# Mixing the keys of batches 2 and 3 with a stationary block matrix and relaying them through a scratch in HBM

## The chip, the cores and the metric

The kernel runs on one core of a Trainium2 chip. The metric is the device time of one execution in microseconds (us). A single execution also gives the span of its profile, which is the time from the first to the last instruction and about 2 us shorter. A run counts as slow when it lies over 1.5% above the fastest run of the same kernel; "same" means within 2%.

## The reference, cut to what matters

```python
# q, k, v: (4 batches, 8 heads, 768 positions, 64); 8 blocks of 96 positions
P = sort_net                      # 5 Sinkhorn rounds make it (nearly) doubly stochastic
k_sorted = einsum('bhij,bhjcd->bhicd', P, k_b)      # mix the 8 blocks of keys, per head
v_sorted = einsum('bhij,bhjcd->bhicd', P, v_b)
attn = softmax(scale * q_b @ k_sorted_b^T)          # attention inside each block
x    = (attn @ v_sorted_b)  ->  (3072 tokens, 512)
out  = (silu(x @ w_gate) * (x @ w_val)) @ w_out     # w_gate, w_val: 512 x 1536
```

The kernel cuts the 3072 tokens into eight stages of 384. Stage n is one pass of gate, value and output projection over the tokens of half a batch, and while it runs, the attention of a later half batch is computed in between. "Stage 2" below runs from the first gate matmul of its tokens to the first of stage 3. Changed is how the keys of batches 2 and 3 are mixed, which falls into stage 2. Their first use is in stage 4.

## The kernel before: the parts that matter here

The matmuls here sum over the partitions. The natural layout of the keys of a pair of batches is (batch, head, block) on the 128 partitions and (position, 64 dims) along the row. For the scores, the 64 dims must lie on the partitions. The kernel before mixes and turns in one step: each matmul takes 128 x 64 keys as the stationary operand and the mixing matrix as the moving one, so the dims come out on the partitions.

```python
def kq_chunk(b, at, n, eng, tag):           # n positions; two output halves of 64 dims
    ...
    for lc in range(n):
        for two in range(2):
            nc.tensor.matmul(tp[two * D:(two + 1) * D, lc, :],
                             lhsT=kq_tiles[b][:, at + lc, :], rhs=rm[:, two], start=True, stop=True)
    drain(eng, dst[:, :, at:at + n], tp.transpose([0, 2, 1]))
```

Pairs of such chunks, 64 matmuls, stand together three times in stage 2. The queries of batches 2 and 3 need no mixing. They already go through HBM and a transposing DMA:

```python
def q_cast(b):      # HBM to HBM, float32 to bfloat16, positions outermost
    nc.gpsimd.dma_start(out=q_scr[b - 2].rearrange("s (h d) -> s h d", d=D),
                        in_=q[b].rearrange("h s d -> s h d"))
def q_dma(b):
    dst = kqt_tile("q")[:, (b - 2) * GI * C:(b - 1) * GI * C]
    nc.sync.dma_start_transpose(out=dst.rearrange("p (g s) -> p g s", g=H2), in_=q_scr[b - 2])
```

The attention outputs of each unit (tile st) reach the feed-forward through another transposing DMA on the same queue, SyncE's:

```python
def x_dma(b, u):
    ...
    nc.sync.dma_start_transpose(out=xts[(b, half)][:, g, :].rearrange("p (i c) -> p i c", c=C),
                                in_=sts.pop((b, u)).rearrange("p i two d -> p (i two d)"))
...
merge(ffn(2), units(1, range(4, 8), (0.0, 5.5)) + kqs("p", (13.0, 16.2, 19.4))
      + [(13.0, lambda: q_dma(2)), (16.4, lambda: q_dma(3))])
```

The softmax here doesn't subtract the row's maximum and nothing guards it: scores larger than these inputs give would overflow.

Of the kernel before, what the change touches and what calls it, by code (L numbers as in the profile page):

```python
# [10 lines left out]
BF16 = mybir.dt.bfloat16  # L11
# [6 lines left out]
def kernel(  # L18
# [11 lines left out]
    nc = tc.nc  # L30

    B, H, S, D = q.shape
    NB = sort_net.shape[-1]
    C = S // NB
    BH = B * H
    H2 = H // 2
# [7 lines left out]
    R = H * NB  # L44
# [10 lines left out]
    natp = ctx.enter_context(tc.tile_pool(name="natp", bufs=2))  # L55
# [13 lines left out]
    warm_sb = const.tile([128, 512], BF16)  # L69
# [9 lines left out]
    nc.vector.memset(e_all[:, :, 4 * C:], 0.0)  # L79

    dram = ctx.enter_context(tc.tile_pool(name="dram", bufs=1, space=bass.MemoryType.DRAM))
    q_scr = [dram.tile([S, H * D], BF16, name=f"q_scr{b}") for b in range(2, B)]
    kq_tiles = {}
    v_tiles = {}
# [32 lines left out]
    def copy_v(eng, pair, rows, s, n=4, d0=0, d1=D):  # L117
        cs = slice(s * (C // n), (s + 1) * (C // n))
        dst = vch3[rows, d0:d1, cs]
        src = v_tiles[pair][rows, cs, d0:d1]  # L120
        if eng is nc.scalar:
            eng.copy(dst, src.transpose([0, 2, 1]))
        else:
            eng.tensor_copy(dst, src.transpose([0, 2, 1]))  # L124
# [4 lines left out]
    ET = mybir.EngineType  # L129
    man = tc.manual_schedule(engines={ET.PE, ET.Pool, ET.DVE, ET.Activation})  # L130
# [23 lines left out]
    rmix = {b: const.tile([128, 2, H, NB], BF16, name=f"rmix{b}") for b in (0, 1, "p")}  # L154
# [21 lines left out]
    def pair_tile(name, tag):  # L176
        return psum.tile([128, 1024], FP32, name=name, tag=tag)

    def bank_tile(name, tag="gen"):
        return psum.tile([128, 512], FP32, name=name, tag=tag, bufs=3 if tag == "gen" else 1)  # L180
# [28 lines left out]
    def drain(eng, dst, src):  # L209
        if eng == "v":  # L210
            nc.vector.tensor_copy(dst, src)  # L211
        else:
            nc.scalar.copy(dst, src)  # L213
# [3 lines left out]
    def kqt_tile(b):  # L217
        if b not in kqts:
            kqts[b] = kqp.tile([128, 2 * H2 * NB * C + 32], BF16, name=f"kqt{b}", tag="kqt")
        return kqts[b]  # L220

    GI = H2 * NB
# [26 lines left out]
    def v_pair_chunk(pair, at, n, eng, tag):  # L249
# [6 lines left out]
                             start=True, stop=True)  # L256
        drain(eng, dst[:, :, at:at + n], tp[0:C].transpose([0, 2, 1]))

    es, sts, xts = {}, {}, {}
    ecount = [0]  # L260

# [30 lines left out]
    def qk(b, u, tag="b"):  # L292
        exps(b, u, *scores(b, u, tag))
# [48 lines left out]
# [3 lines that stand above are left out]
# [66 lines left out]
    idle_ps = bank_tile("idle_ps", "x")  # L411

    def fill(tile, n):
        for _ in range(n):
            nc.tensor.matmul(tile, lhsT=warm_sb[:, 0:128], rhs=warm_sb, start=True, stop=True)

    for _ in range(109):
        nc.tensor.matmul(idle_ps[0:32, 0:32], lhsT=warm_sb[:, 0:32], rhs=warm_sb[:, 0:32],
                         start=True, stop=True)
    for it, n in ((1, 3), (2, 4), (3, 4), (4, 4)):  # L420
        nc.tensor.matmul(idle_ps[0:NB, 0:NB], lhsT=rowreds[it][:, :, 0], rhs=rowreds[it][:, :, 0],
                         start=True, stop=True)
# [10 lines left out]
    def mix_of(dst, b, w):  # L433
        lo = (b % 2) * R
        nc.vector.tensor_tensor(dst, mask[lo:lo + R].unsqueeze(2).to_broadcast([R, H, NB]),
                                w[lo:lo + R].transpose([0, 2, 1]), op=ALU.mult)
# [21 lines left out]
    for b in range(1, B):  # L458
        rows = highr if b % 2 else lowr
        mix_of(rmix["p"][rows, b % 2] if b > 1 else rmix[1][rows, 0], b, w_sb[:, :, b // 2])  # L460
    fill(idle_ps, 3)
    qk(0, 0, "a")
    qk(0, 1, "b")
    qk(0, 2, "gen")
    idle_ps = bank_tile("idle_ps")
# [40 lines left out]
    gate_out(0, 1, first[2])  # L506
    nc.vector.tensor_copy(rmix[1][lowr, 1].rearrange("p h i -> p (h i)"), ident[lowr, lowr])
    man.__exit__(None, None, None)
    man = tc.manual_schedule(engines={ET.PE, ET.Pool})
    man.__enter__()  # L510

    def units(b, us, ats):
        us = list(us)
        todo = []
        for n, at in enumerate(ats):
            u, u2 = us[2 * n:2 * n + 2]
            held = []
            todo.append((at, lambda u=u, u2=u2, held=held: (qk(b, u, "b"), held.append(scores(b, u2, "a")))))
            todo.append((at + 1.3, lambda u2=u2, held=held: exps(b, u2, *held[0])))
            for w, tag, t in ((u, "b", 1.9), (u2, "a", 3.6)):  # L520
                if b == 0 or b == 1 and u < H2:
                    todo.append((at + t, lambda w=w, tag=tag: av(b, w, tag)))
                    todo.append((at + t + 3.1, lambda w=w: drain("v", *xtr(b, w))))
                else:
                    todo.append((at + t, lambda w=w, tag=tag: (av(b, w, tag), x_dma(b, w))))
        return todo

    def kqs(b, ats):
        return [(at, lambda n=n: (kq_chunk(b, n * 32, 16, "v", "b"), kq_chunk(b, n * 32 + 16, 16, "s", "a")))
                for n, at in enumerate(ats)]  # L530

    def vs(f, size, ats):
        return [(at, lambda m=m: f(1, m * size, size, "sv"[m % 2], "ba"[m % 2])) for m, at in enumerate(ats)]

    def merge(main, side):
        done, k = 0.0, 0
        side = sorted(side, key=lambda t: t[0])
        for c, f in main:
            f()
            done += c  # L540
            while k < len(side) and side[k][0] <= done:
                side[k][1]()
                k += 1
        while k < len(side):
            side[k][1]()
            k += 1

    def ffn(n):
        todo = []
        for m in range(NFC):  # L550
            if n > 0 or m > 1:
                todo.append((0.65, lambda m=m: gate(n, m)))
            if n > 0 or m > 0:
                todo.append((0.65, lambda m=m: value(n, m)))
            ends = (5, 8, 11) if n == 1 else (3, 7, 11)
            if n > 0 and m in ends:
                for part in range(3):
                    todo.append((0.87, lambda t3=ends.index(m), part=part: outp(n - 1, t3, part)))
        return todo
# [8 lines left out]
    both = slice(0, 128)  # L568
    merge(ffn(0), units(0, range(4, 8), (0.0, 5.6)))
    merge(ffn(1), vs(v_chunk, 16, (2.2, 3.1, 4.0, 4.9)) + kqs(1, (5.8, 8.0, 10.2)) + units(1, range(4), (11.3, 15.8)))  # L570
    for s in range(4):
        copy_v(nc.gpsimd, 1, both, s)
    nc.vector.memset(kqt_tile("p")[:, 2 * GI * C:], 0.0)
    merge(ffn(2), units(1, range(4, 8), (0.0, 5.5)) + kqs("p", (13.0, 16.2, 19.4))
          + [(13.0, lambda: q_dma(2)), (16.4, lambda: q_dma(3))])
    merge(ffn(3), vs(v_pair_chunk, 8, [1.15 * n for n in range(8)]) + units(2, range(4), (9.8, 14.0)))
    merge(ffn(4), units(2, range(4, 8), (0.0, 8.0)))
    merge(ffn(5), units(3, range(4), (0.0, 8.0)))
    merge(ffn(6), units(3, range(4, 8), (0.0, 8.0)))
# [36 lines left out]
```

## Time and profile before

| | before |
|---|---|
| time, median of 4 runs in the rounds with the change | 250.97 us (250.1 to 253.65) |
| span of the profiled run | 248.4 us |
| TensorE (PE) busy | 237.0 us, 95% |
| stage 2, stage 3 | 29.38 us, 29.69 us |

The prediction below shows the busy shares, the chain and the costs of the pieces. Two more rows of the page matter for what follows. In both, each digit is a fortieth of the span: the clock that TensorE was granted, and the mean busy share of the 16 DMA engines, in tenths.

```profile
PEclk9999999999999999999999999999999999999999
DMA  5949999999999399110112121112111111100122
```

### The profile page before, as it was taken

How to read it: one execution, taken by the hardware profiler on the slowest of the kernel's cores; microseconds unless marked ns; L12 is line 12 of the kernel's file. 1: busy time of each engine (PE TensorE's matmuls, PEld its weight loads, DVE VectorE, ACT ScalarE, POOL GpSimd, SP SyncE). 2: the span in 40 equal slices, each digit the busy share in tenths (PEclk: the TensorE clock that was granted, in tenths of full speed). 3: DMA queues.
4: the chain of work that ended last, by engine and by line, in shares of the span. 5: the costliest groups of instructions: out<-in, count | busy, mean ns of one | idle time of the engine just before them, and what ended most of it. 6: DMA issues, size and time to landing. Idle time of an engine off the chain costs nothing.

```text
span 248.4 us, 5998 instructions
## 1 busy us (share of the span) xinstructions
PE 237.0 (95%) x2528; PEld 141.9 (57%) x2552; DVE 157.6 (63%) x332; ACT 110.4 (44%) x187; POOL 52.7 (21%) x47
## 2 busy tenths in 40 slices
PE   6698999999999999999999999999999999999995
PEld 5285565665555556666655655565555565555543
DVE  6787689785665775857558647755764585446700
ACT  2987552454444444445642552354244344232311
POOL 7948549970059200000000000000000000000000
PEclk9999999999999999999999999999999999999999
DMA  5949999999999399110112121112111111100122
GB/s 98 211 83 167 216 188 227 195 227 214 225 164 191 59 186 156 36 42 3 42 41 67 48 70 33 44 45 74 35 43 42 37 57 57 42 20 26 42 83 89
DMA packets 39530, 24.38 MB, mean 98 GB/s; under 512 B 27728, under 2 KB 35664, under 8 KB 38992
## 3 DMA queue, kind: packets, MB, share of 16 engines
q0 software_dynamic: 21328, 14.16, 38.9%
q1 hardware_dynamic: 18176, 9.84, 15.3%
q8 instruction: 20, 0.33, 0.5%
q14 instruction: 6, 0.05, 0.1%
HBM read 28.32 MB, written 7.86 MB: 146 GB/s over the span
## 4 chain that ended last, share of the span: by engine, by line
PE 73%; DMA 12%; POOL 6%; DVE 4%; issue 3%; ACT 1%; DVEq 0%; POOLq 0%
PE o_ps L389 22%; PE v_ps L372 21%; PE g_ps L354 20%; DMA wv_sb<-in_moe_w_val_dram 5%; DMA kq<-in_k_dram 5%; POOL vch L124 3%; PE tkq L233 3%; DMA wg_sb<-in_moe_w_gate_dram 3%; PE av_ps L303 2%; PE qk L276 2%; PE tv L255 1%; DVE st L309 1%; PE o_ps L405 1%; DVE gs_sb L364 1%; DVE h L377 1%
## 5 line engine op out<-in xcount | busy, mean ns | idle before, releaser
L364 DVE SCALAR_TENSOR_TENSOR gs_sb<-th_sb,g_ps 128x384 bf16<-128x384 bf16 x96 | 52.8, 550 | 54.5 <-ACT th_sb L362 52.2
L372 PE MATMUL v_ps<-xt,wv_sb 128*128 128x384 bf16 x380 | 77.5, 326 | 1.1 <-issue 0.6
L354 PE MATMUL g_ps<-xt,wg_sb 128*128 128x384 bf16 x376 | 76.5, 326 | 0.0
L362 ACT ACTIVATE th_sb<-g_ps 128x384 bf16<-128x384 f32 x96 | 47.2, 492 | 57.3 <-PE g_ps L354 54.9
L389 PE MATMUL o_ps<-wo_sb,h 128*128 128x512 bf16 x255 | 61.9, 379 | 1.2 <-issue 0.2
L377 DVE SCALAR_TENSOR_TENSOR h<-v_ps,gs_sb 128x384 bf16<-128x384 f32 x96 | 53.3, 556 | 6.6 <-PE v_ps L372 0.2
L372 PEld LDWEIGHTS <-wv_sb 128*128 128x128 bf16 x380 | 35.6, 97 | 25.2 <-issue 2.1
L354 PEld LDWEIGHTS <-wg_sb 128*128 128x128 bf16 x376 | 34.5, 97 | 22.6
L389 PEld LDWEIGHTS <-h 128*128 128x128 bf16 x276 | 26.2, 98 | 28.2
L394 ACT COPY o_sb<-o_ps 128x512 f32<-128x512 f32 x23 | 13.5, 587 | 48.7 <-PE o_ps L389 48.7
L124 POOL COPY vch<-v 64x1536 bf16<-64x1536 bf16 (+2 forms) x11 | 28.8, 2652 | 20.5 <-PE g_ps L354 17.0
L289 ACT ACTIVATE e_all<-qk 96x768 bf16<-96x768 f32 x30 | 22.6, 803 | 10.3 <-PE qk L276 10.3
L309 DVE TENSOR_TENSOR st<-av_ps,r_sb 96x512 bf16<-96x512 f32 x32 | 21.7, 679 | 0.2
L303 PEld LDWEIGHTS <-e_all 96*128 96x128 bf16 x256 | 12.2, 98 | 5.0 <-ACT e_all L289 0.9
L303 PE MATMUL av_ps<-vt,e_all 96*128 96x65 bf16 x256 | 13.5, 194 | 0.3 <-ACT e_all L289 0.2
L213 ACT CAST vt<-tv 96x1024 bf16<-96x1024 f32 (+1 forms) x9 | 9.2, 1034 | 4.1 <-PE tv L255 2.6
L307 DVE RECIPROCAL r_sb<-av_ps 96x8 f32<-96x8 f32 x32 | 6.3, 198 | 7.0 <-PE av_ps L303 7.0
L211 DVE CAST vt<-tv 96x1024 bf16<-96x1024 f32 (+1 forms) x9 | 9.8, 1100 | 1.3 <-PE tv L245 1.3
L211 DVE CAST kqt<-tkq 128x1024 bf16<-128x1024 f32 (+1 forms) x7 | 7.4, 1067 | 2.5 <-PE tkq L233 2.4
L233 PE MATMUL tkq<-rmix,kq 128*64 128x64 bf16 x384 | 7.6, 197 | 0.5 <-DVE vt L211 0.4
L213 ACT CAST kqt<-tkq 128x1024 bf16<-128x1024 f32 (+1 forms) x7 | 6.0, 894 | 4.4 <-PE tkq L233 4.4
L233 PEld LDWEIGHTS <-kq 128*64 128x64 bf16 x384 | 6.7, 113 | 2.1 <-issue 2.0
(74 smaller groups left out, 128.4 us busy)
## 6 DMA issues: line engine op xcount, KB each, us to landing
out_dram<-o_sb SPq DMA_DIRECT2D x23, 256.0 KB, 2.0
v<-in_v_dram POOLq DMA_DIRECT2D x3, 768.0 KB, 19.5
kq<-in_q_dram POOLq DMA_DIRECT2D x2, 768.0 KB, 13.7
wg_sb<-in_moe_w_gate_dram POOLq DMA_DIRECT2D x6, 256.0 KB, 8.5
wv_sb<-in_moe_w_val_dram POOLq DMA_DIRECT2D x6, 256.0 KB, 9.1
wo_sb<-in_moe_w_out_dram POOLq DMA_DIRECT2D x1, 1536.0 KB, 23.8
kp<-in_k_dram POOLq DMA_DIRECT2D x2, 768.0 KB, 14.4
q_scr<-in_q_dram POOLq DMA_DIRECT2D x2, 768.0 KB, 29.8
```

The costliest lines, as they stand in the source:

```text
L124: eng.tensor_copy(dst, src.transpose([0, 2, 1]))
L211: nc.vector.tensor_copy(dst, src)
L233: nc.tensor.matmul(tp[two * D:(two + 1) * D, lc, :], lhsT=kq_tiles[b][:, at + lc, :], rhs=rm[:, two], start=True, stop=True)
L289: nc.scalar.activation(e_all[:, n:n + 2, 0:4 * C], wide[0:C, :, 0:4 * C], AF.Exp, scale=scale)
L303: nc.tensor.matmul(o[:, two, i4, :], lhsT=e[:, i4 * C:i4 * C + 128], rhs=vt[:, 2 * g + two, half * 4 + i4, :], start=True, stop=True)
L309: nc.vector.tensor_tensor(st.rearrange("p i two d -> p two i d"), o[0:C, :, :, 0:D], r_sb.to_broadcast([C, 2, 4, D]), op=ALU.mult)
L354: nc.tensor.matmul(g_ps, lhsT=wg_sb[:, kc, ts(m, 128)], rhs=xt[:, kc, :], start=(kc == 0), stop=(kc == NKC - 1))
L362: nc.scalar.activation(th_sb, g_ps, AF.Tanh, scale=0.5)
L364: nc.vector.scalar_tensor_tensor(gs_sb, th_sb, 1.0, g_ps, op0=ALU.add, op1=ALU.mult)
L372: nc.tensor.matmul(v_ps, lhsT=wv_sb[:, kc, ts(m, 128)], rhs=xt[:, kc, :], start=(kc == 0), stop=(kc == NKC - 1))
L377: nc.vector.scalar_tensor_tensor(h_tiles[n][:, m, :], v_ps, 0.5, gs_tiles.pop(m), op0=ALU.mult, op1=ALU.mult)
L389: nc.tensor.matmul(o_ps, lhsT=h_w[:, m, ts(t3, 128)], rhs=wo_sb[:, m, :], start=(m == 0), stop=(m == NFC - 1))
```

## The change

The intent is to spend less TensorE time on the keys. The mixing matrix becomes the stationary operand and the keys stream past it, 512 columns at a time: 12 matmuls in place of 192. The result keeps the layout (batch, head, block) x (position, dim). It is drained, written to a scratch in HBM with positions outermost, and read back by a transposing DMA, as the queries are. Units of attention move later in stages 2 and 3, and SyncE's DMAs are put into program order.

```diff
+    def k_pair_chunk(at, eng, tag):
+        ...
+        for lo in range(0, 1024, 512):
+            nc.tensor.matmul(tp[:, lo:lo + 512], lhsT=rmix["p"].rearrange("p u h i -> p (u h i)"),
+                             rhs=src[:, at + lo:at + lo + 512], start=True, stop=True)
+        drain(eng, k_mixed[0][:, at:at + 1024], tp)
+    def k_out(b):
+        nc.gpsimd.dma_start(
+            out=k_scr[b - 2].rearrange("(i c) (h d) -> h i c d", c=C, d=D),
+            in_=k_mixed[0][(b - 2) * R:(b - 1) * R].rearrange("p (c d) -> p c d", d=D))
+    def k_dma(b):
+        dst = kqt_tile("p")[:, (b - 2) * GI * C:(b - 1) * GI * C]
+        nc.sync.dma_start_transpose(out=dst.rearrange("p (g s) -> p g s", g=H2), in_=k_scr[b - 2])
...
-    man = tc.manual_schedule(engines={ET.PE, ET.Pool})
+    man = tc.manual_schedule(engines={ET.PE, ET.Pool, ET.SP})
...
-    for s in range(4):
+    for s in range(3):
         copy_v(nc.gpsimd, 1, both, s)
...
-    merge(ffn(2), units(1, range(4, 8), (0.0, 5.5)) + kqs("p", (13.0, 16.2, 19.4))
-          + [(13.0, lambda: q_dma(2)), (16.4, lambda: q_dma(3))])
-    merge(ffn(3), vs(v_pair_chunk, 8, [1.15 * n for n in range(8)]) + units(2, range(4), (9.8, 14.0)))
+    merge(ffn(2), [(at, lambda m=m: k_pair_chunk(m * 1024, "vssvss"[m], "ba"[m % 2]))
+                   for m, at in enumerate((0.0, 1.2, 2.4, 3.6, 4.8, 6.0))]
+          + [(6.1, lambda: (k_out(2), k_out(3)))] + units(1, range(4, 8), (7.4, 13.0))
+          + [(18.0, lambda: q_dma(2)), ...])
+    copy_v(nc.gpsimd, 1, both, 3)
+    merge(ffn(3), vs(v_pair_chunk, 8, [1.15 * n for n in range(8)]) + units(2, range(4), (11.5, 16.0))
+          + [(0.5, lambda: q_dma(3)), (6.0, lambda: k_dma(2)), (22.5, lambda: k_dma(3))])
```

(Also changed: 3 filler matmuls before the first scores become 23 small ones.)

More of the change, by code (lines that the diff above doesn't have):

```diff
@@ L81 @@
     dram = ctx.enter_context(tc.tile_pool(name="dram", bufs=1, space=bass.MemoryType.DRAM))
+    k_scr = [dram.tile([S, H * D], BF16, name=f"k_scr{b}") for b in range(2, B)]
     q_scr = [dram.tile([S, H * D], BF16, name=f"q_scr{b}") for b in range(2, B)]
@@ L257, in v_pair_chunk @@
         drain(eng, dst[:, :, at:at + n], tp[0:C].transpose([0, 2, 1]))
+    k_mixed = []
+    def k_pair_chunk(at, eng, tag):
+        if not k_mixed:
+            k_mixed.append(natp.tile([128, C * D], BF16, name="kmix", tag="nat"))
+        src = kq_tiles["p"].rearrange("p c d -> p (c d)")
+        tp = pair_tile("tn", tag)
+        for lo in range(0, 1024, 512):
[9 more added lines that the diff above has]
+        nc.sync.dma_start_transpose(out=dst.rearrange("p (g s) -> p g s", g=H2), in_=k_scr[b - 2])
     es, sts, xts = {}, {}, {}
@@ L415, in fill, with dots @@
             nc.tensor.matmul(tile, lhsT=warm_sb[:, 0:128], rhs=warm_sb, start=True, stop=True)
-    for _ in range(109):
-        nc.tensor.matmul(idle_ps[0:32, 0:32], lhsT=warm_sb[:, 0:32], rhs=warm_sb[:, 0:32],
-                         start=True, stop=True)
+    def dots(n):
+        for _ in range(n):
+            nc.tensor.matmul(idle_ps[0:32, 0:32], lhsT=warm_sb[:, 0:32], rhs=warm_sb[:, 0:32],
+                             start=True, stop=True)
+    dots(109)
     for it, n in ((1, 3), (2, 4), (3, 4), (4, 4)):
@@ L460 @@
         mix_of(rmix["p"][rows, b % 2] if b > 1 else rmix[1][rows, 0], b, w_sb[:, :, b // 2])
-    fill(idle_ps, 3)
+    dots(23)
     qk(0, 0, "a")
@@ L570 @@
     merge(ffn(1), vs(v_chunk, 16, (2.2, 3.1, 4.0, 4.9)) + kqs(1, (5.8, 8.0, 10.2)) + units(1, range(4), (11.3, 15.8)))
-    for s in range(4):
+    for s in range(3):
         copy_v(nc.gpsimd, 1, both, s)
-    nc.vector.memset(kqt_tile("p")[:, 2 * GI * C:], 0.0)
-    merge(ffn(2), units(1, range(4, 8), (0.0, 5.5)) + kqs("p", (13.0, 16.2, 19.4))
-          + [(13.0, lambda: q_dma(2)), (16.4, lambda: q_dma(3))])
-    merge(ffn(3), vs(v_pair_chunk, 8, [1.15 * n for n in range(8)]) + units(2, range(4), (9.8, 14.0)))
+    kqt_tile("q")
+    merge(ffn(2), [(at, lambda m=m: k_pair_chunk(m * 1024, "vssvss"[m], "ba"[m % 2]))
+                   for m, at in enumerate((0.0, 1.2, 2.4, 3.6, 4.8, 6.0))]
+          + [(6.1, lambda: (k_out(2), k_out(3)))] + units(1, range(4, 8), (7.4, 13.0))
+          + [(18.0, lambda: q_dma(2)),
+             (20.0, lambda: nc.vector.memset(kqt_tile("p")[:, 2 * GI * C:], 0.0))])
+    copy_v(nc.gpsimd, 1, both, 3)
+    merge(ffn(3), vs(v_pair_chunk, 8, [1.15 * n for n in range(8)]) + units(2, range(4), (11.5, 16.0))
+          + [(0.5, lambda: q_dma(3)), (6.0, lambda: k_dma(2)), (22.5, lambda: k_dma(3))])
     merge(ffn(4), units(2, range(4, 8), (0.0, 8.0)))
```

## The prediction

> **What bounds the kernel now.** I read the page first: the busy shares, the slices and the chain that ended last.
>
> ```profile
> PE 237.0 (95%) x2528; PEld 141.9 (57%) x2552; DVE 157.6 (63%) x332; ACT 110.4 (44%) x187; POOL 52.7 (21%) x47
> ...
> PE   6698999999999999999999999999999999999995
> ...
> DVE  6787689785665775857558647755764585446700
> ...
> PE 73%; DMA 12%; POOL 6%; DVE 4%; issue 3%; ACT 1%; DVEq 0%; POOLq 0%
> ```
>
> TensorE is busy in nearly every slice and owns 73% of the chain; the DMA and POOL shares lie in the first 48 us (weights and values arriving), which the change leaves alone. A busy PE is not yet a bound PE, so I then read the windows by stage (columns: stretch, length, PE, weight loads, DVE, ACT, POOL, clock, DMA share, GB/s):
>
> ```profile
> 82.00:107.50 25.50, 25.34 (x344) 15.13 (x346) 17.10 (x31) 10.54 (x17) 0.59 (x1) 1.00 0.57 100
> 107.50:134.00 26.50, 26.25 (x244) 16.59 (x245) 18.46 (x34) 14.47 (x23) 0.00 (x0) 1.00 0.14 42
> 134.00:159.80 25.80, 25.64 (x196) 14.61 (x198) 15.81 (x33) 10.51 (x20) 0.00 (x0) 1.00 0.18 51
> ```
>
> In the touched stages PE is idle for only 0.2 us in each 26. Their length is the sum of PE work, so removed PE time counts in full, and DVE (about 67%) has little room for bunched work. Third, the chain in order of time gives what each PE piece costs (start, us, what):
>
> ```profile
> 93.36 1.13 PE tkq L233 x64
> ...
> 97.83 1.13 PE tkq L233 x64
> 98.96 0.76 PE v_ps L372 x4
> 99.72 0.65 PE g_ps L354 x4
> ...
> 108.13 0.45 PE tv L255 x8
> 108.57 0.65 PE v_ps L372 x4
> ...
> 219.20 2.59 PE o_ps L389 x12
> ```
>
> A gate or value group is 0.65 us, but 0.76 right behind a burst of 64 key matmuls: the old path costs 1.13 + 0.11 each time. A burst of eight 128-column matmuls (tv) costs 0.45 and no surcharge. Twelve 512-column matmuls take 2.59 us, 0.216 each.
>
> **What the Trainium skill says.** (1) "TensorE: Matmul & The Clock Gate", section "Wait — 56ns, not 53.3ns?": warm matmuls follow each other at N / 2.4 GHz plus about 2.5 ns, 215.7 ns at N = 512, and never under about 25 ns. The 0.216 us agrees. The floor does not hold here: 64 key matmuls in 1.13 us are 17.7 ns each; they alternate between the two output halves. The trace decides, and it matters: with 25 ns the old path would look 1.4 us dearer than it is. (2) "VectorE: DVE Perf Modes", section "Why PSUM operands drop a tier": a float32 PSUM operand leaves DVE at its base mode. So a contiguous destination should not make the drains cheaper. The trace agrees, as the groups below show. (3) "DMA: Bandwidth & Descriptors", sections "DMA Transpose (X-bar)" (2-byte data, SP or ACT queue only, into SBUF) and "Two DMAs through the same engine are not ordered": a read of scratch must wait for the write's completion. The trace has the same pattern already for the queries; the build shows the same waits for the keys.
>
> ```profile
> L211 DVE CAST kqtp<-tkq 128x1024 bf16<-128x1024 f32 x3 | 3.6, 1216 | 0.0
> ...
> L213 ACT CAST kqtp<-tkq 128x1024 bf16<-128x1024 f32 x3 | 3.0, 1013 | 3.3 <-PE tkq L233 3.3
> ```
>
> The ACT copies to contiguous outputs take 587 ns for 512 columns and 373 for 256: 0.836 ns a column, so 587 + 512 x 0.836 = 1015 ns for 1024, equal to the scattered 1013.
>
> **The change part by part.**
> Removed: three bursts of 64 key matmuls, 3 x (1.13 + 0.11) = 3.72 us of PE, and six drains (3 DVE, 3 ACT).
> Added on PE: 12 matmuls of 512 columns, 12 x 0.216 = 2.59 us. Net on PE -1.13 us, all of it in a PE-bound stage. (128-column groups show no surcharge; I assume none here.)
> Drains: again six of 1024 columns, now 2 on DVE and 4 on ACT: DVE -1.2 us, ACT +1.0 us, neither a bound in sum. They move to the head of stage 2 (ffn(2), starting at 78.1 in the trace), one behind every 0.43 us of PE instead of two behind 1.13. Walking the built order with row durations: the first drain on DVE (about 79.3 to 80.5) stands ahead of the first gate's product, which ends near 81.05, and the fourth gate/value group, which takes over that PSUM buffer, would start at 80.9. That is a wait of about 0.2 us. The later reuses come out with 0.1 to 0.4 us to spare. The value mixing of stage 3 has the same pattern (0.45 us of PE, then a 1.2 us drain) and its chain shows no wait.
> Added on the DMA side: two 0.79 MB scratch writes in 128-byte pieces, two more transposed reads. Measured relatives:
>
> ```profile
> q_scr<-in_q_dram POOLq DMA_DIRECT2D x2, 768.0 KB, 29.8
> ...
> 85.78 4.90 SPq L344 DMA_TRANSPOSE kqtq<-q_scr  x1
> ...
> 92.72 3.46 SPq L344 DMA_TRANSPOSE kqtq<-q_scr  x1
> ```
>
> The 29.8 us is mostly queueing behind 3 MB of loads: in the windows the queue runs dry at 82, and the two query writes land at about 77 and 82, so one takes some 5 to 7 us. The last key drain ends near 88; with 3 us of issue (3.2 for the query writes), the key writes should land by about 97 and 103. The first transposed key read is needed near 121.4 (there the first scores of batch 2 start now; two main groups more ahead of them add 1.3, the saving takes 1.1). On SP, in program order, come: the last attention transpose near 102, the first query read (4.9 us of issue), an output store at 107, the second query read (3.5), then the key read near 112, landing 7 us after issue: about 119. It is hidden, with 2 us of slack. The second key read is issued near 134 and needed near 145.
> Moved: units of batch 1 later in stage 2, those of batch 2 later in stage 3. In stage 3 two things tighten. The second pair of score matmuls there already waits 0.3 us for the DVE to free its PSUM tile (chain: PE to DVE st at 126.7, back to PE at 127.4); the new order puts 0.65 instead of 0.86 us of PE in between: +0.2. And the last attention unit now precedes stage 4 by 3.5 us of PE instead of 5.4. From its matmuls to the end of its DVE work is 1.65 us, the transpose lands 2.3 later, total 4.0; stage 4 touches it at 0.49 us. 3.5 + 0.49 against 4.0: a draw, say +0.1.
> The idle filling before the first scores goes from 3 matmuls of 512 (0.65 us) to 23 dots (109 dots took 3.1 us, so 0.65 us). The scores there wait for a DVE drain that ends at 19.3 us, after both: 0.
> Sum: -1.13 + 0.2 + 0.2 + 0.1 = -0.6 us.
>
> **The rivals.** First, a new wait takes the saving's place: the key read comes late. For it: three big transposes in a row on one queue, never seen back to back in this trace (7 us apart there), and an SP queue that no longer reorders. Against: 2 us of slack, and the scratch is ready some 10 us before the read is issued. If one of them took 10 us, batch 2's scores would wait 1 to 4 us: 251 to 254. Second, DVE and ACT become the bound at the head of stage 2: four ACT drains and gate activations share a ring of three PSUM buffers. If each of the six drains cost 0.2 us instead of one, the saving is gone: 251. Third, a clean gain: no waits at all, plus the surcharge behind other groups falling away: -1.3 to -1.6 us, 249.0. Fourth, the intent read naively: 192 matmuls become 12, so something like 4 us is saved. Against it stands the 17.7 ns of an old matmul.
>
> **Range and chances.** Before: three runs from 250.1 to 253.65, the profiled one 250.42; I take 250.5 as the undisturbed time, because two of the three and the profiled one lie there. Less 0.6 gives 249.9. The clean gain and half a microsecond of spread set the low end at 248.5; a wait of 1 to 1.5 us for the key read sets the high end at 252.0. Faster by over 2% would take 5 us, more than all the key mixing of these batches costs (3.7): 0.02. Slower by over 2% needs a key read some 7 us late: 0.04. Within 2%: 0.94.
>
> **What would show it right or wrong.** PE instructions fall by about 160 (180 key matmuls net, 20 dots back). The new mixing should show 12 matmuls of 512 columns in pieces of 0.43 us. Stage 2 should last 28.2 to 28.6 us instead of 29.4 (78.09 to 107.48 now), its PE idle under 0.5. The drains should still last 1.2 us on DVE and 1.0 on ACT. The key writes should land before 105, the first key read before 121, and no score matmul should wait for a DMA. Stage 4's first gate group should lengthen by 0.1 at most. The prediction is wrong if stage 3 grows by over 1 us (late key read), if PE idles 1 us at the head of stage 2 (drains), or if the span falls below 246.5 (PE cost misread).

## More of the kernel before

The clock is never taken back, and from slice 17 on (about 100 us) the DMA engines are nearly idle. The same is seen in the windows of stages 2 and 3 (stretch, length, then busy time of PE, weight loads, DVE, ACT and POOL, clock, DMA share, GB/s):

```profile
77.93:107.31 29.38, 29.22 (x386) 17.52 (x388) 19.26 (x35) 13.47 (x22) 4.66 (x2) 1.00 0.74 109
107.31:137.00 29.69, 29.38 (x258) 18.10 (x260) 19.95 (x36) 14.81 (x23) 0.00 (x0) 1.00 0.14 41
```

PE idles 0.16 us in stage 2 and 0.31 us in stage 3.

## The result, and the profile after

The changed kernel takes 279.83 us (median of 4 runs, 274.03 to 283.22), against 250.97 us. The ratio of the fast runs is 1.0976, with a 95% interval of 1.0784 to 1.1168: slower. Ratios in this document are the mean time of one kernel's fast runs over that of the other's in the same rounds, so they are not quite the ratio of the medians. Two of the four runs count as slow (283.22 and 281.76), and the profile is of one of these. The fast ones, 274.03 and 277.9, have spans of 272.2 and 276.1 us. I therefore take from this profile where the time goes, and rest nothing on the 5 to 9 us by which its span exceeds those of the fast runs; experiment e2 gives a fast run with the same writes.

The page of the changed kernel, the rows that answer to those of before:

```profile
PE 245.6 (87%) x2392; PEld 143.1 (51%) x2392; DVE 156.8 (56%) x331; ACT 111.4 (40%) x188; POOL 60.3 (21%) x49
...
PE   6988999989999983699303999999999999999994
...
PEclk9999999999999997979955899999999999999999
DMA  6979999999990499899998127120111121110012
...
PE 48%; DMA 29%; POOL 9%; issue 9%; DVE 3%; POOLq 1%; ACT 1%; ACTq 0%
```

PE has holes in slices 15 to 17 and 20 to 22, its clock is lowered in and after them, and the chain has passed from PE (73% to 48%) to DMA (12% to 29%). From slice 15 to 22 the DMA engines are 80 to 90% busy or more; before, they had fallen to 20% or less from slice 17 on. The windows say the same by stage:

```profile
79.48:115.97 36.49, 30.44 (x210) 16.20 (x208) 17.99 (x35) 14.30 (x23) 8.67 (x3) 0.95 0.70 81
115.97:168.78 52.81, 33.67 (x261) 19.85 (x260) 20.45 (x36) 14.92 (x23) 3.65 (x2) 0.81 0.91 69
168.78:194.50 25.72, 25.61 (x197) 14.46 (x196) 15.60 (x32) 10.37 (x19) 0.00 (x0) 1.00 0.31 78
```

Stage 2 has grown by 7.1 us and stage 3 by 23.1 us; stage 4 lasts about what it did. In stage 3 the DMA packets take 0.91 of the time of the 16 engines and yet move only 69 GB/s; in stage 2 of the kernel before, 109 GB/s took 0.74. The experiments below ask whether the small pieces do this.

PE's timeline, the lines with the three large waits (start, us, what, and in brackets the idle time before it with its releaser):

```profile
109.93 1.44 PE L394 MATMUL v_ps<-xt,wv_sb 128*128 128x384 bf16 x4 [5.36 <-DVE kqtp L603]
...
119.67 0.91 PE L256 MATMUL tv<-rmixp,vch 128*128 128x128 bf16 x8 [2.89 <-POOL vch L125]
...
152.44 0.82 PE L298 MATMUL qk<-kqtq,kqtp 64*128 64x96 bf16 x16 [15.77 <-DMA kqtp<-k_scr]
```

The last is the scores of batch 2, which wait for the transposed keys. The first is a wait at second hand. The engine named is DVE, but DVE itself had stood still for 5.3 us:

```profile
108.73 0.69 DVE L331 TENSOR_TENSOR st<-av_ps,r_sb 96x512 bf16<-96x512 f32 x1 [5.32 <-DMA xt<-st]
```

It waits for the transposing DMA of an older st tile, to get the buffer back. Now the two queues. GpSimd's timeline shows the key writes, SyncE's the transposes (us is the issue, not the transfer), and after them stand the rows on the landings: shortest, median and longest time from issue to landing of the two key writes, then KB each and median of two:

```profile
90.59 3.84 POOL L273 DMA_DIRECT2D k_scr<-kmix  x1 [9.22 <-ACT kmix L214]
...
113.03 3.83 POOL L273 DMA_DIRECT2D k_scr<-kmix  x1 [18.59 <-issue]
116.78 2.84 POOL L125 COPY vch<-v 128x1536 bf16<-128x1536 bf16 x1
```

```profile
96.00 7.15 SPq L357 DMA_TRANSPOSE xt<-st  x2
...
105.22 6.07 SPq L357 DMA_TRANSPOSE xt<-st  x2
111.39 3.36 SPq L366 DMA_TRANSPOSE kqtq<-q_scr  x1
...
117.20 17.28 SPq L366 DMA_TRANSPOSE kqtq<-q_scr  x1
134.59 14.44 SPq L279 DMA_TRANSPOSE kqtp<-k_scr  x1
...
168.47 3.24 SPq L279 DMA_TRANSPOSE kqtp<-k_scr  x1
```

```profile
DMA to landing us min/median/max: 22.1/29.2/36.2
...
k_scr<-kmix POOLq DMA_DIRECT2D x2, 768.0 KB, 29.2
...
kqtq<-q_scr SPq DMA_TRANSPOSE x2, 19.2
kqtp<-k_scr SPq DMA_TRANSPOSE x2, 11.5
```

The two key writes land 22.1 and 36.2 us after their issue (the shorter and the longer of the two). If the first takes the shorter, it lands at 90.59 + 22.1 = 112.7, and the second's issue, held for 18.6 us, starts just then, at 113.0. (The kept trace also has a record of each DMA packet, which no view prints one by one. In it the first write's packets are over at 111.7, and the second's run from 117.5 to 148.4.) The value copy that stands behind it on GpSimd comes late, which is the second of PE's waits. On SyncE, the issue of a transpose takes 3.2 to 3.4 us where no key write is in flight (at 111.39, between the two, and at 168.47). Beside a write, two xt transposes take 6 to 7 us instead of 3.3 (at 82.33 in the trace of before), and two single large ones 17.28 and 14.44 us. A long issue is not yet a slow transfer: it can also be held by the transfer before it. From issue to landing these two took 31.4 and 17.8 us, the longer of the two of each of the last rows.

After each wait TensorE also runs at half its clock for a while. The chain in order of time shows it behind the longest one:

```profile
134.59 17.80 DMA kqtp<-k_scr
152.44 0.82 PE qk L298 x16
153.26 1.39 PE g_ps L376 x4
154.65 1.28 PE v_ps L394 x4
```

A group of four that takes 0.65 us elsewhere takes 1.28 and 1.39 here, and the granted clock of this stretch is 0.50. The sum over the 32.8 us by which the span grew (281.2 - 248.4): the three waits are 5.4 + 2.9 + 15.8 = 24.1 us. The half clock behind them, worked out from the chain and, for the first wait, from the timeline as the excess of each group over its usual time, is 1.5 + 1.8 + 2.5 = 5.8 us. Stage 2 also begins 1.6 us later (79.48 against 77.93), before any of the change but the fillers acts; in e2 below, with the same fillers, it begins at 77.44, so this is scatter between runs. That leaves 1.3 us for all the rest, the saving of PE work included.

### The profile page after: what moved, and what is told of

Read it like the earlier page. It is cut to its first block, busy times and chain, and to the rows that moved or that the text cites. A ratio compares the mean times of both kernels' runs of the same rounds, so it can differ in the third digit from the quotient of the medians.

```text
span 281.2 us, 5711 instructions
## 1 busy us (share of the span) xinstructions
PE 245.6 (87%) x2392; PEld 143.1 (51%) x2392; DVE 156.8 (56%) x331; ACT 111.4 (40%) x188; POOL 60.3 (21%) x49
## 3 DMA queue, kind: packets, MB, share of 16 engines
HBM read 28.32 MB, written 9.44 MB: 134 GB/s over the span
## 4 chain that ended last, share of the span: by engine, by line
PE 48%; DMA 29%; POOL 9%; issue 9%; DVE 3%; POOLq 1%; ACT 1%; ACTq 0%
PE o_ps L411 15%; PE v_ps L394 14%; PE g_ps L376 13%; DMA q_scr<-in_q_dram 10%; DMA kqtp<-k_scr 6%; DMA wv_sb<-in_moe_w_val_dram 5%; DMA kq<-in_k_dram 4%; POOL vch L125 3%; POOL k_scr L273 3%; DMA wg_sb<-in_moe_w_gate_dram 2%; PE tv L256 1%; PE av_ps L325 1%; PE qk L298 1%; POOLq L641 1%; PE o_ps L427 1%
## 5 line engine op out<-in xcount | busy, mean ns | idle before, releaser
L394 PE MATMUL v_ps<-xt,wv_sb 128*128 128x384 bf16 x380 | 79.6, 333 | 6.1 <-DVE kqtp L603 5.4
L376 PE MATMUL g_ps<-xt,wg_sb 128*128 128x384 bf16 x376 | 78.3, 331 | 0.5 <-DVE h L399 0.4
L411 PE MATMUL o_ps<-wo_sb,h 128*128 128x512 bf16 x276 | 65.2, 383 | 1.2 <-DMA wo_sb<-in_moe_w_out_dram 1.0
L394 PEld LDWEIGHTS <-wv_sb 128*128 128x128 bf16 x380 | 36.4, 99 | 31.3 <-issue 8.7
L331 DVE TENSOR_TENSOR st<-av_ps,r_sb 96x512 bf16<-96x512 f32 x32 | 21.8, 680 | 5.6 <-DMA xt<-st 5.3
L298 PE MATMUL qk<-kqtq,kqtp 64*128 64x96 bf16 x128 | 4.6, 213 | 15.9 <-DMA kqtp<-k_scr 15.8
L273 POOL DMA_DIRECT2D k_scr<-kmix x2 | 7.7, 3838 | 27.8 <-issue 18.6
L298 PEld LDWEIGHTS <-kqtp 64*128 64x128 bf16 x128 | 3.2, 99 | 18.9 <-DMA kqtp<-k_scr 16.2
```

The costliest lines, as they stand in the source:

```text
L273: nc.gpsimd.dma_start(out=k_scr[b - 2].rearrange("(i c) (h d) -> h i c d", c=C, d=D), in_=k_mixed[0][(b - 2) * R:(b - 1) * R].rearrange("p ...
L331: nc.vector.tensor_tensor(st.rearrange("p i two d -> p two i d"), o[0:C, :, :, 0:D], r_sb.to_broadcast([C, 2, 4, D]), op=ALU.mult)
L376: nc.tensor.matmul(g_ps, lhsT=wg_sb[:, kc, ts(m, 128)], rhs=xt[:, kc, :], start=(kc == 0), stop=(kc == NKC - 1))
L394: nc.tensor.matmul(v_ps, lhsT=wv_sb[:, kc, ts(m, 128)], rhs=xt[:, kc, :], start=(kc == 0), stop=(kc == NKC - 1))
L411: nc.tensor.matmul(o_ps, lhsT=h_w[:, m, ts(t3, 128)], rhs=wo_sb[:, m, :], start=(m == 0), stop=(m == NFC - 1))
```

## The experiments

The theory (A): the scratch writes are slow by themselves, because 6144 pieces of 128 bytes fall on only 8 of the 16 DMA engines, and while they move, every transposing DMA is slowed beside them. The rivals: three large transposes in a row, or SyncE's program order, are what is slow (B); the key read waits for its write by dependence (C); the write is slow only because it meets the transposes (D). Kernels ran with the kernel before beside them: its median was 250.53 us (7 runs) for e1 to e4, 250.53 us (7 runs) for e5 to e8, and 250.62 us (11 runs) for e9 to e11. All profiles below are of fast runs.

One caution: the on-chip comparison with the reference passed for every run, also where the keys are wrong. With q and k of size 0.1 the scores are close to zero and the softmax is nearly flat, so this comparison does not guard the keys. That the changed kernel, e5, e9 and e10 put every key in its place follows from the index arithmetic of their edits; the experiments called wrong measure time alone.

### e1: no scratch write; the key reads read the queries' scratch

```diff
-    ... dma_start_transpose(out=..., in_=k_scr[b - 2])
+    ... dma_start_transpose(out=..., in_=q_scr[b - 2])
-          + [(6.1, lambda: (k_out(2), k_out(3)))] + units(1, range(4, 8), (7.4, 13.0))
+          + units(1, range(4, 8), (7.4, 13.0))
```

The keys are wrong; all else of the change stays, the three transposes in a row and SyncE's order too.

> The changed kernel without the two scratch writes of the mixed keys; the key transposes read the query scratch instead, so the result is wrong on purpose. SyncE's program, the three large transposes in a row, the unit positions and the PE work stay. Theory A (the two scratch writes, while in flight, occupy the DMA engines and stretch every transpose beside them): the time falls to 249 to 250.5 us, each large transpose is issued in 3.3 to 5 us and lands in about 7, no score matmul waits for a DMA. Theory B (three large transposes behind each other on an in-order SyncE are slow by themselves): the second and third still take over 10 us each and the time stays above 258.

Measured: 251.52 us (4 runs, 251.05 to 253.69), ratio 1.0044 (0.9963 to 1.0125). SyncE's timeline:

```profile
93.85 2.90 SPq L357 DMA_TRANSPOSE xt<-st  x2
...
99.89 3.17 SPq L357 DMA_TRANSPOSE xt<-st  x2
103.16 3.30 SPq L366 DMA_TRANSPOSE kqtq<-q_scr  x1
...
108.15 4.46 SPq L366 DMA_TRANSPOSE kqtq<-q_scr  x1
112.71 3.18 SPq L279 DMA_TRANSPOSE kqtp<-q_scr  x1
```

With the writes gone, so are all the long issues and all three waits; the four large transposes land 5.2 to 7.0 us after their issue. Theory B falls: the transposes stand in the same order and the same row. The gain of the change does not appear either; the time lies above the 249 to 250.5 expected, which is taken up at e11.

### e2: the writes stay, nobody reads them

```diff
-    ... dma_start_transpose(out=..., in_=k_scr[b - 2])
+    ... dma_start_transpose(out=..., in_=q_scr[b - 2])
```

> The writes as in the changed kernel (8 x 8 x 96 pieces of 128 bytes), but nothing reads them: the key transposes read the query scratch, wrong result on purpose. Theory A (occupied DMA engines): as slow as the changed kernel, 270 to 284 us, second query transpose and first key transpose still 10 us or more of issue. Theory C (what costs is the dependence of the key transposes on the writes, the wait for their completion): below 256. It is also the base of the next two runs.

Measured: 275.17 us (2 runs), ratio 1.0959 (1.0866 to 1.1053), much the same as the change. PE's waits are 5.0, 4.0 and 8.5 us, the last for a key read that depends on no key write. Its issue:

```profile
114.86 4.80 SPq L366 DMA_TRANSPOSE kqtq<-q_scr  x1
119.75 18.58 SPq L279 DMA_TRANSPOSE kqtp<-q_scr  x1
```

Landing of the query transposes (median of two), in e2 and in e1:

```profile
kqtq<-q_scr SPq DMA_TRANSPOSE x2, 15.0
...
kqtq<-q_scr SPq DMA_TRANSPOSE x2, 6.9
```

Theory C falls: the transposes are slow beside the writes, not because of them. In the change itself the first transpose issued after the second write's issue took 17.28 us to issue; here, where that write is issued at 111.75, the one at 114.86 was issued in 4.80, but it landed only after 22.7 us (the longer of the two), and the next, whose issue took 18.58, after 25.3.

### e3 and e4: one property of the write changed at a time

Both write the same bytes to another place, so both have wrong keys. e3 keeps the 128-byte pieces and makes the outermost dimension 64. e4 keeps an outermost dimension of 8 and writes pieces of 12288 bytes.

```diff
 # e3
-    out=k_scr[b - 2].rearrange("(i c) (h d) -> h i c d", c=C, d=D)
+    out=k_scr[b - 2][:, :, 0:D]             # scratch of R=64 x C=96 x 512
 # e4
-    out=k_scr[b - 2].rearrange("(i c) (h d) -> h i c d", c=C, d=D)
+    out=k_scr[b - 2][:, 0:NB, :]            # scratch of H=8 x (NB+1) x C*D
```

> As e2, but the scratch is laid out so that the write's outermost dimension is 64 rows instead of 8 heads; the pieces are still 128 bytes at a step of 1024 bytes. Wrong result on purpose. Theory A1 (a DMA is spread over as many engines as divide its outermost dimensions, so 8 of 16 in the change): each write takes about half as long as in e2, 9 us instead of 18 to 22 from end of issue to landing, its second issue on GpSimd no longer waits some 18 us, and the time falls to 250 to 258. Theory A2 (the 128-byte pieces are what is slow, on any number of engines): unchanged from e2, above 268.

> As e2, with outermost dimension 8 as in the change, but pieces of 12288 bytes instead of 128 (a scratch row per partition). Wrong result on purpose. Theory A1 (number of engines is all that counts): as slow as e2. Theory A2 (small pieces): the writes land in under 8 us each, the transposes keep their 3.3 to 5 us, the time is 249 to 252. If both halve the time, piece size and engine count multiply.

Measured: e3 261.03 us (2 runs), ratio 1.0396 (1.0307 to 1.0486), outside what I had expected. e4 251.72 us (2 runs), ratio 1.0025 (0.994 to 1.0111). In e3 the writes land 16.0 us after issue (median of the two), the second's issue is no longer held, and the large transposes are back at 3.3 to 3.7 us. What is left is at the xt transposes:

```profile
94.09 5.70 SPq L357 DMA_TRANSPOSE xt<-st  x2
...
101.50 10.12 SPq L357 DMA_TRANSPOSE xt<-st  x2
```

They bring an 8.3 us wait of PE in stage 2, by way of DVE and its st buffers. In e4 the writes land 9.9 us after issue (under 8 was expected), and two xt transposes take 4.48 us in the pair issued beside the writes (2.90 in e1) and 3.17 in the next. So the large pieces do not spare a transpose beside them; they are over sooner. By the packet records, the writes move from 95.1 to 111.7 and from 117.5 to 148.4 us in the change, for 18.7 us in e3 and for 8.3 us in e4, where the two run together and are over at 97.8. All large transposes of e3 and e4 come after that. What a large transpose would suffer beside a write in large pieces, no run here shows.

### e5: the real scratch, with an outermost dimension of 16

One write for both batches, into a scratch of 768 x 1024; the result is correct.

```diff
-    out=k_scr[b - 2].rearrange("(i c) (h d) -> h i c d", c=C, d=D), in_=k_mixed[0][(b - 2) * R: ...]
+    out=k_scr.rearrange("(i c) (u h d) -> (u h) i c d", c=C, h=H, d=D), in_=k_mixed[0]...
```

> The changed kernel made correct on 16 engines: one scratch of 768 x 1024, heads of both batches side by side, so that batch and head merge into an outermost dimension of 16; one write of 12288 pieces of 128 bytes; the key transposes read their half of it. Theory A1+A2 (engine count and piece size both count, as the four runs before say): like the sixteen-engine run e3, 256 to 264 us, the write landing 15 to 22 us after its issue, attention transposes of batch 1 still 5 to 10 us for two. If e3's gain came from its spread-out rows (no two pieces in one 512-byte block) and not from the engines: 268 us or more.

Measured: 261.23 us (2 runs), ratio 1.0417 (1.0355 to 1.048). The write of 1.57 MB lands 23.8 us after its issue. The 19 us of wait of the key scores and of the value mixing are gone; PE still waits 7.0 us in stage 2. The outermost dimension, with one write in place of two, takes the ratio from 1.0976 to 1.0417, a little over half of the loss.

### e6: the writes by themselves

The kernel before, with three extra writes to unused scratches in stages 6 and 7, where no transpose is due: the change's own shape (8 outermost, 128 bytes), e5's (16, 128 bytes) and e4's (8, 12288 bytes).

```diff
+    merge(ffn(6), units(3, range(4, 8), (0.0, 8.0)) + [(18.0, lambda: gated(6, 7, write8))])
+    merge(ffn(7), [(11.0, lambda: gated(7, 5, write_large)), (17.0, lambda: gated(7, 8, write16))])
```

> The kernel before, with three extra writes of its unmixed keys to unused scratch in the last two stages, where no transpose is in flight: the change's write of 8 x 768 pieces of 128 bytes (0.79 MB), then the same bytes in 12288-byte pieces with outermost dimension 8, then 16 x 768 pieces of 128 bytes (both batches, 1.57 MB). Time 250 to 252.5 (they are hidden). Theory A (the write is slow by itself): the first lands 20 us or more after issue, as in the changed kernel (22). Theory D (write and transposes slow each other down): the first lands within 14 us of issue (3.8 of it issue), the second within 8, the third within 22.

Measured: 258.68 us (2 runs), ratio 1.0316 (1.0232 to 1.04). This time was a miss: the program does not end before its last write has landed, and I had put that write near the end. What the run was for are its DMA lines (KB each, us from issue to landing):

```profile
w_scr<-kp POOLq DMA_DIRECT2D x1, 1536.0 KB, 22.2
...
w_scr<-kp POOLq DMA_DIRECT2D x1, 768.0 KB, 21.8
wl_scr<-kp POOLq DMA_DIRECT2D x1, 768.0 KB, 9.4
```

With no transpose near it, the change's write takes 21.8 us, as in the change. Theory D falls as it stands: the write is slow by itself. The two do slow each other, though: the second write of the change and of e2, beside large transposes, landed after 36.2 and 31.1 us, and both writes of e7, whose transposes stand in another order, after 20 to 21. The issue of the quiet write took 3.85 us, so the data needed about 18.0 us; e5's write, with twice the bytes, took 22.2 us, of which 3.80 are issue. If the first uses 8 engines and the second 16, each engine carries 6144 / 8 = 12288 / 16 = 768 pieces in both, and a piece costs 18.0 / 768 = 23 ns in the one and 18.4 / 768 = 24 ns in the other. (These are estimates from the two rows.) The third row sets the pieces' size apart: the same bytes on 8 outermost, in 12288-byte pieces, took 9.4 us, of which 0.58 are issue. Large pieces and 16 outermost each about halve the 18.0 us of 0.79 MB, to 8.8 and to 18.4 / 2 = 9.2. The Trainium skill states the rule behind the "if". In "DMA: Bandwidth & Descriptors", section "Why a DMA increments its semaphore by 16 and not by 1", a DMA is spread over the largest number up to 16 that divides the slowest dimension, other than 1, of both of its access patterns. For 8 heads against 64 partitions that is 8; for 16 against 128 it is 16. The equal times agree with it, and so do the packet records: of the packets of 4096 bytes (32 pieces), 8 are open at once for 7.6 us of the change's write and more than 8 for under 0.1 us, against 16 for 3.6 us of e5's.

### e7: SyncE not in program order

```diff
-    man = tc.manual_schedule(engines={ET.PE, ET.Pool, ET.SP})
+    man = tc.manual_schedule(engines={ET.PE, ET.Pool})
```

> The changed kernel with SyncE's order left to the scheduler again, as before the change; the built order now puts both query transposes ahead of the key writes and the first key transpose between the second and third attention transpose of batch 1. If program order of SyncE is a cause of the loss: under 262 us. If the writes are: 270 us or more, because the first key transpose still waits for or runs beside a write and now also holds up the attention transposes behind it.

Measured: 276.33 us (2 runs), ratio 1.102 (1.0956 to 1.1083). The wait only changes its place. A key transpose now stands ahead of xt transposes, and the gate matmuls of stage 3 wait for these (PE's waits: us in total, times, longest):

```profile
PE g_ps L376 <- DMA xt<-st: 16.5, 2, 15.0
```

The program order on SyncE is neither the cause nor a cure.

### e8: e5 with eight st buffers instead of three

```diff
-    ssp = ctx.enter_context(tc.tile_pool(name="ssp", bufs=3))
+    ssp = ctx.enter_context(tc.tile_pool(name="ssp", bufs=8))
```

> e5 with 8 instead of 3 buffers for the attention output tiles, so that a slow attention transpose no longer keeps the DVE, and through it the PE, waiting for a free tile. In e3 that wait was 8.2 us, 8.3 of PE idle. Theory E (that buffer wait is how the slow transposes reach the PE when the key reads themselves are in time): 250 to 254 us and no DVE wait for an attention transpose. If instead the next stage's gate matmuls wait for the late attention tile: only a few us better than e5.

Measured: 261.18 us (4 runs), ratio 1.0429 (1.0384 to 1.0474), the same as e5. DVE's wait for a buffer is gone, and PE waits 6.6 us for the xt tiles themselves. The buffers only passed the delay on.

### e9: large pieces and correct keys

The scratch is laid out so that one partition's row is one piece: 64 pieces of 12288 bytes per write, 64 outermost. For that, the mixed keys must hold two heads' dims side by side, so each 512-column matmul fills only 64 rows and there are 24 of them, and a key transpose now reads 3072 rows of 128.

```diff
+    k_scr = dram.tile([2, H2, NB, C, 2 * D], BF16, name="k_scr")
+    for two in range(2):
+        for half in range(2):       # 24 matmuls in all, lhsT of 64 columns
+            nc.tensor.matmul(tp[half * R:(half + 1) * R, two * 512:(two + 1) * 512], lhsT=rmt[:, two], rhs=...)
+    out=k_scr.rearrange("u g i (half c) e -> half (u g i) (c e)", half=2)[b - 2]
```

> The change with another layout of mixed keys and scratch and the same schedule: each pair of heads is mixed into one partition, so that a partition's bytes are one run of the scratch (12288-byte pieces, 64 of them a write, outermost dimension 64), and a key transpose reads 3072 rows of 128. 24 matmuls of 512 columns and 64 rows that alternate between the output halves, instead of 12 of 128 rows. Theory A (piece size and engine count are the whole loss): each write lands within 10 us, no PE wait for a DMA in stages 2 and 3, 250.5 to 252.5 us, like e4. If halves do not overlap at 512 columns: 2.6 us more. If the transposed read of 256-byte rows is slow: above 255.

Measured: 252.41 us (4 runs, 251.44 to 253.64), ratio 1.0068 (1.0029 to 1.0107). GpSimd issues both writes in one go, and they land 7.6 us after issue (median):

```profile
88.34 1.10 POOL L278 DMA_DIRECT2D k_scr<-kmix  x2 [8.74 <-ACT kmix L215]
```

No matmul of these stages waits for a DMA. The path through HBM is therefore sound if the piece is large: of a loss of 9.8%, 0.7% is left. The writes are over at 98.1, before the large transposes begin; the xt pair beside them took 5.28 us. The matmuls of the two halves overlap only in part: a chunk of four takes 0.56 us where two full ones took 0.43, and PE is busy 29.68 us in stage 2, more than before (29.22).

### e10: e9 with the attention units in before's places

```diff
-    merge(ffn(2), [... k_pair_chunk ... (0.0, 1.2, 2.4, 3.6, 4.8, 6.0)] + [(6.1, k_out ...)] + units(1, range(4, 8), (7.4, 13.0)) ...)
+    merge(ffn(2), units(1, range(4, 8), (0.0, 5.5)) + [... k_pair_chunk ... (9.6, 11.0, 12.4, 13.8, 15.2, 16.6)]
+          + [(9.2, q_dma(2)), (9.3, q_dma(3)), (16.7, k_out ...)] ...)
```

> e9 with the units of batches 1 and 2 back in the places of the kernel before, the six mixing chunks behind them in stage 2 with drains alternating between DVE and ACT, both query transposes ahead of the writes. It is the version that should beat both: the PE saving of 1.1 us without the drains' waits of e1 (1.3 us in stage 2, 0.3 at stage 4): 249 to 250.2 us against 250.5. If the halves do not overlap or the late write delays the first scores of batch 2: 251 to 254.

Measured: 251.51 us (6 runs, 250.89 to 251.76), ratio 1.0023 (0.9994 to 1.0053). This is the best correct version with the relay, and it does not beat the kernel before; the 249 to 250.2 us expected were missed. With 24 half matmuls PE is busy 29.49 us in stage 2, against 29.22 before, so the saving of PE work was not in it. No run here has both the 12 full matmuls and a write in large pieces.

### e11: e1 with the drains cut to 64 columns

To find where e1's saving went: the drains of the mixed keys become nearly free, and all else is as in e1. The keys are wrong.

```diff
-        drain(eng, k_mixed[0][:, at:at + 1024], tp)
+        drain(eng, k_mixed[0][:, at:at + 64], tp[:, 0:64])
```

> e1 (no writes) with each drain of mixed keys cut from 1024 to 64 columns; wrong result on purpose. In e1 stage 2 lasted 29.6 us, 1.3 more than its PE work. Theory F (the drains at the head of the stage hold up the gate and value PSUM buffers): stage 2 lasts 28.2 to 28.7 and the time is 1 to 1.4 us under e1, 250.1 to 250.6 when the kernel before is at 250.5. Rival (the moved attention units cause it): stage 2 stays at 29.4 to 29.7.

Measured: 251.27 us (4 runs, 250.8 to 253.09), ratio 1.0034 (0.9993 to 1.0074). The windows of stage 2, of e1 and of e11:

```profile
77.33:106.92 29.59, 28.48 (x207) 15.74 (x209) 17.99 (x35) 14.29 (x23) 5.51 (x2) 1.00 0.53 77
```

```profile
80.05:109.06 29.01, 28.32 (x206) 15.76 (x208) 16.17 (x35) 11.30 (x23) 5.22 (x2) 1.00 0.32 66
```

Stage 2 lasts 29.01 us in e11, between what the two expectations named. PE idles 1.11 us of stage 2 in e1 and 0.69 us in e11, against 0.16 us before. Two of e1's waits, on PE's timeline:

```profile
85.27 1.02 PE L411 MATMUL o_ps<-wo_sb,h 128*128 128x512 bf16 x4 [0.43 <-DVE h L399]
...
91.50 0.81 PE L394 MATMUL v_ps<-xt,wv_sb 128*128 128x384 bf16 x4 [0.28 <-DVE gs_sb L386]
```

The first, an output projection that waits for DVE's h, is gone in e11; the second, 0.28 us, is still there. Stage 3 lasts 29.90 us in both (before 29.69), and the first gate of stage 4 stretches by 0.3 us in both. So the drains cost some 0.6 us of stage 2, and what is left of the saving is lost to the other waits, which fits the moved attention units: from e9 to e10, which puts these back, PE's idle time of stage 2 falls from 0.69 to 0.19 us (the mixing moves too). Each of these is one profile, and the times of e1 and e11 do not differ; the shares are an account.

## Why the prediction was wrong

**The failed step: the size of the key writes.** The prediction took "some 5 to 7 us" for a key write from the landings of the query writes, because both move 0.79 MB in 128-byte pieces. For the query writes it fits: by the packet records of before, the two move in 12.8 us, 6.4 each. The key writes differ in the outermost dimension: 768 positions there, 8 heads here. That is the larger part (18.0 us against 9.2 with 16 outermost, e6); the step from 6.4 to 9.2 is not taken apart (the query writes go from HBM to HBM and convert float32). Measured: 22.1 us in the change and 21.8 us alone (e6), of which 18 move data. "Land by about 97 and 103" became about 112.7 and, if issue and landing pair as above, 149.2. The two sections of the DMA page that the prediction names are about what is allowed and in what order; the one on the number of engines, drawn on at e6, was not held against the diff. Nor was the size of the piece: with 12288 bytes the same data lands in 9.9 and 7.6 us (e4, e9).

**The second failed step: the transposes' own cost.** The working takes 4.9 and 3.5 us of issue and 7 us to landing from a trace in which no such write ran beside them, and then adds them up on a queue beside two writes. The transposes in flight with a write took 17.28 and 14.44 us to issue (18.58 in e2), and 31.4 and 17.8 us to land (22.7 and 25.3 in e2). This is the first rival's direction, a late key read, but neither of the grounds given for it: not three transposes in a row and not SyncE's order (e1, e7). It said "if one of them took 10 us, batch 2's scores would wait 1 to 4 us"; two took over 14, and they waited 15.8 us in the slow run that was profiled, and 8.5 in e2, a fast run with the same writes.

**What the working did not have at all.** The writes also delayed the small xt transposes, and through three st buffers DVE and PE in stage 2 (5.4 us; 8.3 in e3, 7.0 in e5). The held second issue delayed a value copy on GpSimd (2.9 us). And waits cost clock: the Trainium skill, "TensorE: Matmul & The Clock Gate", section "What's actually happening", has the clock halved after an idle window of about 3.4 us, until work has gone on about as long. The trace agrees in kind: 1.28 us for a group of 0.65 behind each of the three waits, 5.8 us in all.

**TensorE's work: right in its pieces.** In the new mixing two matmuls take 0.43 to 0.45 us, as predicted. The groups of the changed kernel (busy, mean ns):

```profile
L214 ACT CAST kmix<-tn 128x1024 bf16<-128x1024 f32 x4 | 4.0, 1012 | 2.8 <-PE tn L268 2.8
...
L268 PE MATMUL tn<-kp,rmixp 128*128 128x512 bf16 x12 | 3.6, 379 | 0.0
L212 DVE CAST kmix<-tn 128x1024 bf16<-128x1024 f32 x2 | 2.4, 1220 | 1.6 <-DMA q_scr<-in_q_dram 1.6
```

The drains last 1.22 us on DVE and 1.01 on ACT: right, and so is the reading that a contiguous destination does not make them cheaper. (379 ns is a matmul's own length; they overlap, and twelve take 12 x 0.216 us of the engine.) PE's matmuls fell by 136 in the records, of which some can be missing, and its weight loads by exactly the 160 named (2552 to 2392). PE's busy time of stage 2 fell by less than the 1.13 us forecast, though: from 29.22 to 28.48 in e1 and 28.32 in e11.

**The small waits: mis-sized.** The sum put 0.2 + 0.2 + 0.1 us against a saving of 1.13. With the writes out of the way (e1), stage 2 lasts 29.59 us, where 28.2 to 28.6 was predicted, stage 3 grows by 0.2 as said, and stage 4's first gate by 0.3 instead of 0.1. The waits of stage 2 are the term that was off: about 1.1 us of idle instead of a few tenths. The third rival, a clean gain, is not seen even with nearly free drains (e11: 1.0034, its interval from 0.9993 up, where -0.6 us would be 0.998). The second rival, 251 us with the drains eating the saving, comes closest to e1, with the drains somewhat under half of it.

**The chances.** "Slower by over 2%" had 0.04, for "a key read some 7 us late". It came 15.8 us late in the profiled run and 8.5 in e2.

What stays open: why a transpose beside such a write slows so much, and what the 23 to 24 ns of one small piece consist of. The packet records show only that it crawls: the 6144 packets of 256 bytes of the second query transpose and the first key transpose are spread over 29.9 us in the change (121.9 to 151.8) and over 26.7 in e2, against 7.3 in e1.

## What to carry to other kernels

Before a relay through HBM is called hidden, work out its writes from their own access pattern: the number of pieces, their bytes, and the outermost dimension that decides over how many engines they spread. A duration may be borrowed from another transfer only if all three agree, and source and destination too, as the 6.4 and 9.2 us above suggest. And a transfer that is off the critical path can still slow those on it, so list what else is in flight on the DMA engines in the same stretch; here the same data cost nearly 10% of the run in 128-byte pieces and under 1% in pieces of 12288 bytes.

## What the Trainium skill lacked or had wrong

- "DMA: Bandwidth & Descriptors": its rule for the number of engines held, but it has no measured time of one small piece in a write from SBUF to HBM, only 512 bytes as the smallest transfer for full rate ("Specifications") and a fixed overhead for each packet in cycles ("Why small descriptors are slow (HBM only)"). Here the cost is about 23 to 24 ns per 128-byte piece and engine (18.0 and 18.4 us for 768 pieces each, e6), worked out with that rule.
- The same page says in "Rules for kernel authors" that a transpose next to ordinary DMAs needs nothing. It speaks there of corrupted data; for time it is not so. Beside a write in 128-byte pieces a large transposed read landed 17.8 to 31.4 us after its issue (the change, e2) instead of 5.2 to 7.0 (e1).
- No page has it that the second of two such writes on GpSimd is held at its issue: 18.6 us in the change, 19.4 in e2 and 17.7 in e7, with GpSimd's later work behind it; with 64 outermost or large pieces it was not (e3, e4, e9). The nearest is a descriptor buffer that can fill up ("Perfetto Trace Analysis", "DMA Instruction — SWDGE (GPSIMD)"); no run shows whether that is it.
- "TensorE: Matmul & The Clock Gate" gives an idle window of about 3.4 us for the lowered clock, and its table at the end about 3 us. A wait of 2.9 us was enough in the change (a group of 1.28 us instead of 0.65 behind it, at a granted clock of 0.50).
- The same page's floor of about 25 ns between matmuls, however small, does not hold for the key matmuls of the kernel before, which alternate between the two output halves: 17.7 ns each. Its Part 3, on packing small matmuls, has tiles of the array work at the same time; the floor does not name that case.
